# Weight pieces issued from ScalarE, four under way, with five slots in the second layer

## The chip, the cores and the metric

The kernel runs on one core of a Trainium2 chip. The metric is the device time of one execution in microseconds (us); the time before is the median of three runs. The engines of the core are TensorE (PE, with its weight loads as PEld), VectorE (DVE), ScalarE (ACT), GpSimd (POOL) and SyncE (SP). They run side by side, each through its own list of instructions in order, and wait for each other through semaphores. Transfers (DMA) are issued from such a list too, and sixteen DMA engines carry them out.

## The reference

What is computed is a causal attention with a decay, and a two-layer network on its output. Inputs have batch 8, 8 heads, 576 positions and head size 64; the network has model width 512 and inner width 2048, on 8 x 576 = 4608 tokens.

```python
def _attn_ref(q, k, v, f):
    scores = scale * np.matmul(q, k.transpose(0, 1, 3, 2))
    cum = np.cumsum(np.log(np.clip(f, 0.0001, 1.0)), axis=-1)
    decay = cum[:, :, :, None] - cum[:, :, None, :]
    scores = np.where(causal, -1000000000.0, scores + decay)
    attn = np.exp(scores - np.max(scores, axis=-1, keepdims=True))
    attn = attn / (np.sum(attn, axis=-1, keepdims=True) + 1e-09)
    return np.matmul(attn, v)

def _moe_ref(x, w_in, w_out):
    h = x @ w_in
    g = h * np.clip(h + 3.0, 0.0, 6.0) / 6.0
    return g @ w_out
```

`x` is the attention's output with the heads put side by side. The two weights come as 64-bit floats, so each is 8 MB.

## The kernel before

**Attention.** It goes over "virtual heads" (list `VH`): four of kind A, which do the first 256 positions of two heads of batch 0 each; eight of kind B, which do the other positions of one head of batch 0; and 56 of kind F, one head each of batches 1 to 7. For each, q and k come into `ST` (`load_x`, L402), are cut into two parts of fewer bits by GpSimd (`parts`, L441, and `rests`, L451, which also sends T<-TQ and T<-TK through DMAs), and rows of the running sums of the decay come into `TK` (`load_c`). For kinds A and B, `natural` (L474) computes scores for the row maxima, `max_rows` (L495) turns the maxima and sends them as a short row to partition 96 of `TQ` (TQ<-mr, L502), and `scores` (L541) computes transposed scores and exponentials. `av` (L679) multiplies by v. `load_v` (L349) loads v of a batch: batch 0 goes into memory of `v16` and `xT`, the other batches into `vst`. The first load of `vst` stands in the program at the seventh head of kind B.

**The two layers.** Tokens are worked on in nine tiles of 512. `h_unit` (L772) makes 128 of the 2048 inner columns: twelve matmuls (L781 to L783), a Relu on ScalarE (L791), a product on VectorE (L794), and the split of the result into a 16-bit float and a rest (L795, L796). `out_unit` (L799) does the second layer, three matmuls (L803 to L805) for each of 16 chunks. Tile 0 is done in two halves of 256 tokens. These units are woven among the attention's steps by `fill`.

**Weights.** Both weights come in 16 pieces of 512 KB each (128 rows of 512 64-bit numbers). A piece is loaded into a slot (`w_load`, L233). `w_decode` (L241) makes 32-bit floats of it: a pass on ScalarE (L250), two on VectorE (L251, L252), and a Square on ScalarE (L256) that writes over the slot and sums the squares. The Square is the last pass over the slot. When all squares of a group of four pieces (first layer) or of all 16 (second layer) are summed, `pow2_scale` gives a scale, and `w_split` (L281) makes two 16-bit floats of each number: the first on ScalarE (L283), the second through TensorE (L286, L287) and ScalarE (L288) or on VectorE (L294).

The first layer has six slots: the three tiles of `ring`, and three pieces of the memory of `w2`, which is not yet in use. The second layer has three, `ring` alone. Later `ring` serves the heads of kind F.

All loads are issued by SyncE. In the first layer four pieces are loaded ahead, then a fifth, and then piece k + 5 is issued ahead of the decode of piece k; the first eight are pinned behind the last of the short rows issued so far (`pinned`, L206). In the second layer three pieces are loaded ahead, in a step of their own, and then piece k + 3 behind the decode of piece k.

**What sets the order.** The program text gives each instruction a place; the steps of the weights (`w_step`) are put among the attention's, eight to a head of kind A, five for B, four for F (`W_RATE`). A planner then simulates the program and sets each engine's list, by place in the program and by when it takes an instruction to be ready, so that instructions can move against the program text. `tc.issue_after` holds an instruction behind a given one on its engine, and `tc.keep_in_program_order` behind the one traced before it on its engine.

Of the kernel before, what the change touches and what calls it, by code (L numbers as in the profile page):

```python
# [13 lines left out]
I32 = mybir.dt.int32  # L14
# [6 lines left out]
def kernel(  # L21
# [10 lines left out]
    nc = tc.nc  # L32
# [52 lines left out]
    F_RATE = (0.6, 0.45, 1.02)  # L85
    PIN = 0
    PIN0 = 1
# [13 lines left out]
    NSP = 3  # L101
    PL_POOL = ((3, ), ())
    NAT = ((1, 4, 0), (2, 3))
    B0_POOL = ((0, 0), (1, 1))
    W_AHEAD = (4, 5)
    W_ORDER = 0
# [24 lines left out]
    vst = cpool.tile([P, NCH, VR], F32, name="vst")  # L131
# [74 lines left out]
    def pinned():  # L206
        return tc.issue_after(small[-1]) if small else nullcontext()


    wide = w_in.dtype == mybir.dt.int64  # L210
    NW = 16
    CW = NCC * DFF // NW
    wsum = cpool.tile([P, 2 * NW], F32, name="wsum")
    ring = [cpool.tile([P, 2 * CW], I32, name=f"ring{i}") for i in range(NRING)]
    gTf = gT.bitcast(F32).rearrange("p a c t -> p (a c t)")
    w2f = w2.bitcast(F32).rearrange("p k a e -> p (k a e)")
    spare = w2.bitcast(I32).rearrange("p k a e -> p (k a e)")
    slots_out = [t[:, :] for t in ring]
    slots_in = slots_out + [spare[:, (2 * h + 9) * CW:(2 * h + 11) * CW] for h in range(NSP)]

# [11 lines left out]

    def w_load(i, k, slots):  # L233
        src, x, _ = w_chunk(i, k)
        with pinned() if PIN or i == 0 and k < 8 else nullcontext():
            if wide:
                nc.sync.dma_start(slots[k % len(slots)], src.bitcast(I32))
            else:
                nc.sync.dma_start(x, src)

# [55 lines left out]
    def w_in_work():  # L296
        first, ahead = W_AHEAD
        for k in range(first):
            w_load(0, k, slots_in)
        yield  # L300
        for k in range(first, ahead):
            w_load(0, k, slots_in)
        for j in range(NG):
            ks = range(j * NCC, (j + 1) * NCC)
            for k in ks:
                if k + ahead < NW:
                    w_load(0, k + ahead, slots_in)
                w_decode(0, k, slots_in)
                yield
            pm = w_gram(ks) if GRAM[j] else w_sum(ks[0], ks[-1] + 1)  # L310
# [13 lines left out]
    def w_out_work():  # L324
        n = len(slots_out)
        for k in range(n):
            w_load(1, k, slots_out)
        yield

        for k in range(NW):  # L330
            w_decode(1, k, slots_out)
            if k + n < NW:
                w_load(1, k + n, slots_out)
            yield
# [579 lines left out]
    for i, (kind, n) in enumerate(VH):  # L914
        b, h = divmod(n, H)
# [4 lines left out]
        ahead = i + 2 < NV  # L920
# [99 lines left out]
```

## Time and profile before

| what | value |
|---|---|
| median of three runs | 1080.63 us (1080.21 to 1082.72) |
| the profiled execution: time | 1083.28 us |
| the profiled execution: span | 1081.5 us |
| mean granted clock of TensorE | 0.982 |
| PE busy | 1010.1 us (93%) |
| DVE busy | 719.7 us (67%) |
| ACT busy | 610.1 us (56%) |
| POOL busy | 413.1 us (38%) |
| read from HBM | 47.93 MB |

A profile is of one execution. L250 is line 250 of the kernel. The busy time of TensorE includes time in which its pipelined matmuls only overlap. SPq is SyncE's list, where a row is the issuing of a transfer, not its flight. In the chain of waits, a row with DMA is the time from an issue to its landing, as far as it released what follows. A name such as `w` stands for all tiles whose names differ in numbers only: `w1` and `w2` are both `w`. "ring<-in_w_out_dram" is a piece of the second layer's weights on its way into a slot.

### The profile page before, as it was taken

Reading aid. Unit: us, or ns where it says so; the run is one execution under the profiler, and the core shown is the slowest. Engines: PE = TensorE matmul, PEld = TensorE weight load, DVE = VectorE, ACT = ScalarE, POOL = GpSimd, SP = SyncE. Lnnn points to the kernel's source line nnn. Section 1 sums busy time; section 2 is a strip of 40 time slices with the busy share of each in tenths; the row PEclk is TensorE's granted clock in tenths of the full one; section 3 lists DMA queues with packets and bytes.
Section 4 is the critical chain, followed back from the end, with each engine's and each line's share of the span. In section 5 each row is a group of like instructions: output and inputs, shape, how many; then the busy total and the mean of one; then the engine's idle time right before and its main releaser. Section 6 shows DMA issues by size and latency. Waiting matters only on the chain.

```text
span 1081.5 us, 20281 instructions
## 1 busy us (share of the span) xinstructions
PE 1010.1 (93%) x7074; PEld 577.4 (53%) x7074; DVE 719.7 (67%) x1887; ACT 610.1 (56%) x1285; POOL 413.1 (38%) x505
## 2 busy tenths in 40 slices
PE   2799977988999999999999989999999999999998
PEld 2567854755555555555555545555555555444443
DVE  7869899876885688468865795689668841510520
ACT  4778656845764577356754674477447841621520
POOL 7344455335434445444544444454445420000000
PEclk9989989999999999999999999999999999999999
DMA  8866547767756666667576856675666651000001
GB/s 258 277 172 194 150 105 134 179 127 150 156 114 141 140 146 118 137 129 164 108 139 138 164 113 130 146 166 114 128 140 128 106 112 46 1 10 30 1 1 39
DMA packets 261650, 133.74 MB, mean 124 GB/s; under 512 B 229444, under 2 KB 231036, under 8 KB 261548
## 3 DMA queue, kind: packets, MB, share of 16 engines
q1 hardware_dynamic: 261548, 132.45, 54.7%
q8 instruction: 56, 0.92, 0.3%
q14 instruction: 46, 0.38, 0.1%
HBM read 47.93 MB, written 9.73 MB: 53 GB/s over the span
## 4 chain that ended last, share of the span: by engine, by line
PE 64%; DVE 12%; DMA 9%; issue 5%; ACT 5%; SPq 2%; POOL 2%; DVEq 0%; POOLq 0%; ACTq 0%
PE po L803 10%; PE po L804 10%; PE po L805 10%; PE ph L781 7%; PE ph L782 7%; PE ph L783 7%; DMA vst<-in_vS_dram 3%; PE pn L611 3%; PE pn L608 2%; DVE pp L619 2%; DVE ring L648 2%; DMA T<-TK 1%; DVE gT L796 1%; DMA w<-in_w_in_dram 1%; DVE r L794 1%
## 5 line engine op out<-in xcount | busy, mean ns | idle before, releaser
L781 PE MATMUL ph<-xT,w 128*128 128x512 f16 (+1 forms) x640 | 231.2, 363 | 14.5 <-DVE r L794 9.1
L782 PE MATMUL ph<-xT,w 128*128 128x512 f16 (+1 forms) x640 | 230.2, 363 | 0.0
L783 PE MATMUL ph<-xT,w 128*128 128x512 f16 (+1 forms) x640 | 230.0, 363 | 0.0
L631 ACT ACTIVATE pp<-pp,nb 128x192 f32<-128x192 f32 x280 | 138.5, 552 | 148.8 <-DVE nb L625 145.8
L804 PE MATMUL po<-w,gT 128*128 128x512 f16 x576 | 216.3, 381 | 6.1 <-DVE w L294 6.1
L805 PE MATMUL po<-w,gT 128*128 128x512 f16 x576 | 215.9, 381 | 0.0
L803 PE MATMUL po<-w,gT 128*128 128x512 f16 x576 | 213.6, 381 | 1.1 <-ACT o L814 0.8
L648 DVE TENSOR_TENSOR ring<-pp,ring 128x128 f16<-128x128 f32 (+2 forms) x216 | 131.5, 622 | 84.1 <-ACT ring L645 83.2
L791 ACT ACTIVATE r<-ph,bias_r,SC 128x256 f32<-128x256 f32 (+7 forms) x272 | 144.4, 570 | 28.6 <-PE ph L783 27.9
L794 DVE SCALAR_TENSOR_TENSOR r<-r,ph 128x512 f32<-128x512 f32 (+1 forms) x160 | 100.1, 627 | 88.9 <-ACT r L791 88.6
L458 POOL TENSOR_TENSOR T<-ST,T 64x576 fp32r<-64x576 f32 (+1 forms) x68 | 101.2, 1488 | 143.2 <-DMA T<-TK 133.4
L619 DVE CUSTOM_DVE_ANT_0 pp<-pn,W 128x192 f32<-128x192 f32 x280 | 122.9, 482 | 20.6 <-PE pn L611 16.6
L796 DVE TENSOR_TENSOR gT<-r,gT 128x512 f16<-128x512 f32 (+1 forms) x160 | 118.3, 743 | 27.4 <-ACT gT L795 26.6
L795 ACT CAST gT<-r 128x512 f16<-128x512 f32 (+1 forms) x160 | 91.8, 575 | 75.9 <-DVE r L794 75.8
L608 PE MATMUL pn<-TK,TQ 68*128 68x192 f32 x336 | 124.1, 383 | 5.8 <-issue 5.0
L611 PE MATMUL pn<-T,T 128*128 128x192 f32 x336 | 113.5, 368 | 4.3 <-POOL T L458 4.3
L645 ACT CAST ring<-pp 128x192 f16<-128x192 f32 x280 | 112.9, 452 | 0.0
L455 POOL TENSOR_TENSOR T<-ST,TQ 64x576 fp32r<-64x576 f32 (+2 forms) x68 | 97.6, 1435 | 24.8 <-PE pn L611 18.2
L654 POOL TENSOR_TENSOR ring<-pp,ring 128x128 f16<-128x128 f32 x96 | 61.5, 641 | 105.5 <-ACT ring L645 83.7
L782 PEld LDWEIGHTS <-w 128*128 128x128 f16 x640 | 62.7, 99 | 65.8 <-issue 20.9
L805 PEld LDWEIGHTS <-gT 128*128 128x128 f16 x576 | 56.8, 99 | 74.9 <-issue 13.7
L781 PEld LDWEIGHTS <-w 128*128 128x128 f16 x640 | 63.1, 99 | 62.2 <-issue 14.3
(136 smaller groups left out, 1703.4 us busy)
## 6 DMA issues: line engine op xcount, KB each, us to landing
ST<-in_qk_dram SPq DMA_DIRECT2D x64, 288.0 KB
T<-TK SPq DMA_DIRECT2D x64, 144.0 KB
out_dram<-o SPq DMA_DIRECT2D x36, 256.0 KB
ring<-in_w_out_dram SPq DMA_DIRECT2D x16, 512.0 KB
T<-TQ SPq DMA_DIRECT2D x56, 144.0 KB
vst<-in_vS_dram SPq DMA_DIRECT2D x7, 1040.0 KB
ring<-in_w_in_dram SPq DMA_DIRECT2D x9, 512.0 KB
w<-in_w_in_dram SPq DMA_DIRECT2D x7, 512.0 KB
```

What stands on the lines that cost most here:

```text
L608: nc.tensor.matmul(dst, TQ[i][0:D + 4, qs], TK[i][0:D + 4, a:e], start=True, stop=False)
L611: nc.tensor.matmul(dst, T7[j][:, qs], T1[j][:, a:e], start=False, stop=True)
L619: nc.vector.tensor_tensor_reduce(pp[:r, w:w + kw], pn[:r, o:o + kw], W[:r, 4 * P + r - kw:4 * P + r], 1.0, -3.0e38, ALU.add, ALU.max, accu ...
L631: nc.scalar.activation(x_, x_, AF.Exp, bias=nb[:r, e0 + x:e0 + x + 1], scale=0.125)
L648: eng.tensor_tensor(hl[:r, a:a + c * P], pp[:r, at[c] + 64:at[c] + kw], hl[:r, h0[c] + 64:h0[c] + kw], op=ALU.subtract,)
L781: nc.tensor.matmul(ph, w1[0][:, cc, fs_], xh, start=(cc == 0), stop=False)
L782: nc.tensor.matmul(ph, w1[0][:, cc, fs_], xl, start=False, stop=False)
L783: nc.tensor.matmul(ph, w1[1][:, cc, fs_], xh, start=False, stop=(cc == NCC - 1))
L791: nc.scalar.activation(r[:, a:e], ph[:, a:e], AF.Relu, bias=bias_r, scale=scol(A1 + NG * b + fc * NG // NFC))
L803: nc.tensor.matmul(po, gT[:, 0, fc, ts_], w2[:, fc, 0, :], start=(fc == 0), stop=False)
L804: nc.tensor.matmul(po, gT[:, 0, fc, ts_], w2[:, fc, 1, :], start=False, stop=False)
L805: nc.tensor.matmul(po, gT[:, 1, fc, ts_], w2[:, fc, 0, :], start=False, stop=(fc == NFC - 1))
```

## The change

- Only the first four loads are issued by SyncE. Each later one is issued by ScalarE, traced behind the decode of a piece: all 32 pieces of both layers form one list, and each decode takes the next from it. So the load of piece k + 4 stands behind the Square of piece k, and the first four pieces of the second layer stand behind the decodes of the last four of the first.
- `tc.keep_in_program_order` holds each of ScalarE's loads behind the instruction traced ahead of it on ScalarE, which is the Square.
- The pinning of the first eight loads behind the short rows, the fifth load ahead, and the step in which the second layer's first three loads were issued are taken out.
- The second layer has five slots: `ring`, and two in the memory of `vst`. The first load of `vst` therefore has to wait for the last use of these two.

```diff
-    W_AHEAD = (4, 5)
+    W_AHEAD = 4
...
-    slots_out = [t[:, :] for t in ring]
-    slots_in = slots_out + [spare[:, (2 * h + 9) * CW:(2 * h + 11) * CW] for h in range(NSP)]
+    vsp = vst.bitcast(I32).rearrange("p c e -> p (c e)")
+    slots_out = [t[:, :] for t in ring] + [vsp[:, 2 * h * CW:2 * (h + 1) * CW] for h in range(2)]
+    slots_in = [t[:, :] for t in ring] + [spare[:, (2 * h + 9) * CW:(2 * h + 11) * CW] for h in range(NSP)]
...
-    def w_load(i, k, slots):
+    loads = [(i, k) for i in range(2) for k in range(NW)]
+
+    def w_load(eng):
+        if not loads:
+            return
+        i, k = loads.pop(0)
         src, x, _ = w_chunk(i, k)
-        with pinned() if PIN or i == 0 and k < 8 else nullcontext():
-            if wide:
-                nc.sync.dma_start(slots[k % len(slots)], src.bitcast(I32))
-            else:
-                nc.sync.dma_start(x, src)
+        slots = (slots_in, slots_out)[i]
+        dst, src = (slots[k % len(slots)], src.bitcast(I32)) if wide else (x, src)
+        d = eng.dma_start(dst, src)
+        if eng is nc.scalar:
+            tc.keep_in_program_order(d)
...
     def w_in_work():
-        first, ahead = W_AHEAD
-        for k in range(first):
-            w_load(0, k, slots_in)
+        for k in range(W_AHEAD):
+            w_load(nc.sync)
         yield
-        for k in range(first, ahead):
-            w_load(0, k, slots_in)
         for j in range(NG):
             ks = range(j * NCC, (j + 1) * NCC)
             for k in ks:
-                if k + ahead < NW:
-                    w_load(0, k + ahead, slots_in)
                 w_decode(0, k, slots_in)
+                w_load(nc.scalar)
                 yield
...
     def w_out_work():
-        n = len(slots_out)
-        for k in range(n):
-            w_load(1, k, slots_out)
-        yield
-
         for k in range(NW):
             w_decode(1, k, slots_out)
-            if k + n < NW:
-                w_load(1, k + n, slots_out)
+            w_load(nc.scalar)
             yield
```

More of the change, by code (lines that the diff above doesn't have):

```diff
@@ L85 @@
     F_RATE = (0.6, 0.45, 1.02)
-    PIN = 0
     PIN0 = 1
```

## The prediction

> **What bounds the kernel now.** I first read the busy times in five stretches of the span, then who TensorE waits for up to 135 us, then the timelines around its longest holes, and last the chain of work that ended last.
>
> A row of the windows gives the stretch, its length, busy time (and instructions) of PE, PEld, DVE, ACT, POOL, then the granted clock, the DMA share and GB/s.
> ```profile
> span 1081.5 us, 20281 instructions
> ...
> 10.00:54.00 44.00, 26.69 (x115) 20.32 (x115) 34.30 (x106) 26.08 (x58) 21.22 (x27) 0.95 0.88 270
> 54.00:136.00 82.00, 77.97 (x556) 62.55 (x557) 65.83 (x183) 59.14 (x125) 36.73 (x39) 0.94 0.58 170
> 136.00:200.00 64.00, 49.86 (x443) 33.23 (x444) 62.52 (x173) 44.34 (x95) 33.95 (x35) 0.95 0.66 138
> ...
> 300.00:1081.00 781.00, 764.18 (x5257) 403.86 (x5255) 473.10 (x1205) 413.67 (x865) 269.50 (x335) 1.00 0.50 105
> ```
> From 300 us on TensorE is busy 764 of 781 us and no weight piece is under way, so the change can't act there except by an order of work that starts earlier or later. From 54 to 136 us it is busy 78.0 of 82. From 136 to 200 VectorE is busy 62.5 of 64 us, and TensorE idles 14.1. The room that touches weight loading is the stretch from 10 to 54 us: 17.3 us idle on TensorE, and its longest two waits up to 135 us are these (total, times, longest):
> ```profile
> PE pn L484 <- DMA TK<-cs: 12.8, 1, 12.8
> PE ps L548 <- DMA TQ<-mr: 7.4, 2, 4.3
> ```
> The 12.8 are the start of the attention and no weight's business. The 7.4 are two waits for a 2 KB row of maxima. The later one is the last row of TensorE's timeline here, and then come issues on SyncE's queue:
> ```profile
> 47.94 0.38 PE L183 MATMUL pt_w<-wm,ones 128*128 128x1 f32 x2 [2.50 <-ACT w L288]
> ...
> 53.04 0.27 PE L499 MATMUL ptm<-identr,MC 128*3 128x128 f32 x1 [1.77 <-DVE MC L490]
> 56.38 0.58 PE L548 MATMUL ps<-TQ,TK 97*128 97x256 f32 x1 [3.07 <-DMA TQ<-mr]
> ```
> ```profile
> 42.39 0.52 SPq L237 DMA_DIRECT2D ring<-in_w_in_dram  x1
> ...
> 46.01 0.33 SPq L237 DMA_DIRECT2D ring<-in_w_out_dram  x1
> ...
> 48.07 0.67 SPq L502 DMA_DIRECT2D TQ<-mr  x1
> ```
> From the first to the second of these rows SyncE issues four weight pieces of 512 KB (the page's list of issues has the size), all in one queue ahead of that small row. The chain says what it costs (start, length, what):
> ```profile
> 14.40 7.06 DMA w<-in_w_in_dram
> 24.99 6.42 DMA w<-in_w_in_dram
> 42.39 4.33 DMA ring<-in_w_in_dram
> 48.07 8.26 DMA TQ<-mr
> 77.89 5.30 DMA ring<-in_w_out_dram
> 90.48 3.96 DMA ring<-in_w_out_dram
> ```
> Up to 95 us the chain runs five times through the flight of a weight piece, 27.1 us in all, and once through 8.26 us for the small row. So early on the kernel is paced by when weight pieces and the small transfers queued among them land.
>
> **The change, part by part.** *SyncE loses 28 of its 32 weight issues, and ScalarE gains them* (four remain on SyncE at the start). Their issues now, by the view of each weight's tile (duration in ns min/median/max):
> ```profile
> L237 SPq DMA_DIRECT2D ring<-in_w_in_dram x9: 327/432/534, 2.0 to 44.8; - x9
> ...
> L237 SPq DMA_DIRECT2D ring<-in_w_out_dram x16: 323/420/1287, 32.8 to 110.7; - x16
> ```
> 28 x 0.42 = 11.8 us leave SyncE, and with them the time in which SyncE stood before a piece whose slot wasn't free, while the attention's transfers queued behind it (from 0 to 200 us):
> ```profile
> SPq L237 <- ACT ring L256: 5.9, 6, 2.0
> SPq L237 <- ACT w L256: 3.3, 2, 2.0
> ```
> The small row of 48.07 us is then in a queue that holds no weights ahead of it. Weight pieces now fly 3.96 us where the queue is shortest (the chain's 90.48), so I expect no more than that of a row of 2 KB: 8.26 - 3.96 = 4.3 us sooner, more than the 3.07. The 1.77 just ahead are a wait for the maxima of the next head, on a VectorE that stands behind the same stall's decodes. I take both, **-4.8 us**. Bounds: -4.84, and 0 if the row is as late as now.
> The Trainium skill ("DMA: Bandwidth & Descriptors", "Queues, rings and completion order") says that each DMA engine takes turns between the queues of SyncE and ScalarE, a packet at a time. By that, the row passes the weights and the term stands; the trace of before has one data queue and cannot show it.
>
> *The clock.* Behind that stall TensorE runs slowly:
> ```profile
> 50.00:60.00 10.00, 5.17 (x22) 4.45 (x22) 4.52 (x20) 6.92 (x14) 3.03 (x3) 0.50 0.68 175
> 60.00:70.00 10.00, 10.00 (x46) 6.11 (x45) 6.80 (x24) 7.09 (x16) 4.11 (x6) 0.84 0.41 119
> ...
> 40.62 0.36 PE L548 MATMUL ps<-TQ,TK 97*128 97x256 f32 x1
> ```
> The matmul of 56.38 us takes 0.58 where the same took 0.36 at 40.62. From 56.4 to 60 us that is 3.6 x 0.38 = 1.4, and 10 x 0.16 = 1.6 in the next ten: 3.0 us if the clock never fell, 0 if it falls all the same. Some idle time will stay there, so half: **-1.5 us**.
>
> *Pieces start earlier.* The fifth to eighth piece are no longer held behind the attention's small transfers: each goes out behind the Square of one of the first four, where now the sixth issue is at 14.40 and the eighth at 24.99 (the chain's first two rows). ScalarE now idles for landings:
> ```profile
> ACT gT L250 <- DMA ring<-in_w_in_dram: 10.2, 6, 5.3
> ACT gT L250 <- DMA w<-in_w_in_dram: 5.3, 3, 2.4
> ACT w L250 <- DMA ring<-in_w_out_dram: 3.9, 5, 1.5
> ...
> 46.74 0.66 ACT L250 ACTIVATE gT<-ring 128x512 f32<-128x512 f32 x1 [0.76 <-DMA ring<-in_w_in_dram]
> ```
> Little of these 19.4 us is on TensorE's path. The one place I can point to is TensorE's 2.50 at 47.94, which waited for an eviction (L288) that stands right behind this decode of 46.74 on ScalarE, and so behind its 0.76. **-0.8 us**; bounds 0 and -2.5. That more pieces are under way doesn't raise the rate where the DMA share is full already:
> ```profile
> 20.00:30.00 10.00, 6.92 (x32) 6.42 (x32) 8.64 (x25) 3.82 (x8) 4.32 (x5) 1.00 1.03 320
> ...
> 19.09 0.43 SPq L354 DMA_DIRECT2D v<-in_vS_dram  x1
> ...
> 24.35 1.75 DVE L365 TENSOR_REDUCE vm<-v 128x1 f32<-128x1536 f32 x1 [0.20 <-DMA v<-in_vS_dram]
> 25.91 2.88 PE L702 MATMUL pav<-v,pf 128*128 128x96 f32 x12
> ```
> There the weights take it from v and the heads. The load of v, issued at 19.09 and landed by 24.35, could at half the rate need 5.3 us more and hold the matmuls of L702, at 25.91 now, by 24.35 + 5.26 - 25.91 = 3.7. Against that, the first small row (the 4.3 of the 7.4) may come sooner by up to half, 2. I take 0, bounds -2 and +3.7.
>
> *ScalarE pays the issues.* 28 x 0.42 = 11.8 us. From 10 to 136 us ScalarE is idle 17.9 + 22.9 = 40.8, which covers them. Behind an issue on ScalarE stand the exponentials (L567), the evictions (L288, L791) and the next decode, and TensorE and VectorE wait for these. Only three issues add a wait: output pieces 0 to 2 go into the slot that the Square just ahead of them has written. Later ones use a slot whose readers were done one piece before. On the path I count those of the stretch from 44 to 56 us, where TensorE is not covered: three, **+1.3 us**. Bounds 0 and 11.8 (if none were covered).
>
> *Five slots in the second layer.* Two lie in vst, so the load of batch 1's v must now wait for the Square of output piece 14 of 0 to 15. At present the last Square but one runs at 113.65 and the load is issued behind a small row of 115.33:
> ```profile
> 113.65 0.63 ACT L256 ACTIVATE ring<-w 128x512 f32<-128x512 f32 x1 [0.26 <-DVE w L252]
> ...
> 115.33 0.75 SPq L502 DMA_DIRECT2D TQ<-mr  x1
> ```
> 1 us of slack as it is, more if the pieces come sooner: 0. If they come later by x, VectorE (which reduces that v) loses x - 1. Decoding earlier gains nothing by itself from 54 to 136 us, where TensorE has 4.0 us of idle left, 3.07 of them already counted; nor from 136 on, where VectorE has the same passes to do: 0.
>
> Sum: -4.8 - 1.5 - 0.8 + 1.3 = **-5.8 us**. The profiled execution took 1083.28 us (span 1081.5), 2.65 above the median of 1080.63; it becomes 1077.5, and the median **1074.8**.
>
> **The rivals.** *A, more:* the second layer's pieces are decoded early enough that VectorE's splits of them also move ahead. TensorE waits for the splits in 136 to 200 us:
> ```profile
> PE po L804 <- DVE w L294: 6.1, 5, 1.8
> ```
> All of it: -5.8 - 6.1 = -11.9, 1068.7. For it: VectorE idles 16.2 us from 54 to 136, room for earlier passes. Against: the splits stand in the program behind steps of the attention.
> *B, nothing:* sharing 16 engines, the small row is as late as now, and the stall with its slow clock stays; -0.8 + 1.3 = +0.5, 1081.1. For it: the share of 1.03 in 20 to 30 us; four weight pieces are always under way, in rows of 512 KB / 128 = 4 KB. Against: in 54 to 136 us the share is 0.58.
> The skill's same page ("Issuing engines are not separate DMA queues") says that issuing from several engines only saves sequencer time, which is B's outcome.
> *C, slower:* ScalarE's issues land on the path. An issue takes up to 1.287 us on SyncE, and ScalarE's stream is in order, so exponentials and evictions come late by the issue and the wait before it. If all 28 count at 0.42: +11.8 - 7.1 = +4.7, 1085.3. It decides from 10.3 us on the path (7.1 gained, 3.2 lost): 25 issues at 0.42, or 8 at 1.287. For it: ScalarE is busy 59.1 of 82 us, in series with VectorE at 65.8. Against: the idle time above. That the whole order is planned anew, and may fall worse, is in the range.
>
> **Chances.** Forecast 0.37, A 0.18, B 0.20, C 0.25. No change is within 0.3% (3.2 us), about what a measurement of this kernel can tell. Forecast and A are faster: 0.55; B the same: 0.20; C slower: 0.25. The likeliest's own range is 1071 to 1078; for 8 in 10 it goes from 1066 (A, with the earlier v and eviction bounds) to 1086 (C).
>
> **What would show it.** A second data queue with some 28 x 512 KB in the page's third section. TensorE's wait for TQ<-mr near 50 us gone and that row landing within 4 us of its issue; the clock in 50 to 70 us above 0.8. ScalarE's waits for weight landings well under 19.4 us, and the last Square of the second layer before 118 us. A is right if L804 no longer waits for L294. C is right if TensorE shows new waits for L567, L288 or L791 that add up to more than 7 us. The prediction is wrong if v lands after 28 us and L702 waits for it, or if the span changes behind 300 us, where I count nothing.

## The result and the profile after

The changed kernel takes 1095.9 us (median; 1093.49 to 1100.15), the kernel before beside it 1081.68 us. The ratio is **1.0129**, 95% interval 1.0085 to 1.0173: the change makes the kernel 1.3% slower. A second measurement of the same change, with more runs, gave 1.0125 (1.0087 to 1.0163). The prediction was 1074.8 us, with a range up to 1086.

In the changed kernel every line behind L400 or so has a number lower by 3 than before: L564 is the exponential (before L567), L699 the product with v (L702), L481 the scores for the maxima (L484), L545 the transposed scores (L548). The weights' loads are at L244, the passes of a decode at L257 to L259 and its Square at L263.

The page of the changed kernel, its span and its queues:

```profile
span 1091.7 us, 20269 instructions
...
q1 hardware_dynamic: 257516, 117.77, 49.2%
q10 hardware_dynamic: 4032, 14.68, 4.6%
```

The second data queue is there: 14.68 MB are 28 pieces of 512 KB. The profiled execution took 1093.49 us, and its span is 10.2 us longer than that of before.

Where the 10.2 us are: the windows view, first of the kernel before and then of the changed one. A row gives the stretch, its length, the busy times (and instructions) of PE, PEld, DVE, ACT and POOL, TensorE's granted clock, the DMA share and GB/s.

```profile
0.00:60.00 60.00, 30.32 (x130) 23.66 (x131) 44.22 (x135) 36.12 (x74) 33.16 (x49) 0.91 0.83 253
60.00:136.00 76.00, 74.35 (x542) 59.21 (x542) 63.83 (x175) 54.47 (x117) 33.70 (x37) 0.98 0.58 174
```

```profile
0.00:60.00 60.00, 24.45 (x100) 17.82 (x100) 42.14 (x122) 32.95 (x68) 31.70 (x46) 0.97 0.84 255
60.00:136.00 76.00, 74.15 (x487) 59.56 (x488) 57.38 (x164) 52.28 (x109) 29.27 (x33) 0.87 0.59 164
...
300.00:1091.00 791.00, 773.48 (x5313) 409.14 (x5311) 477.05 (x1215) 419.78 (x879) 272.62 (x341) 0.99 0.50 106
```

Busy time times clock is the work that TensorE did, in us at full clock. Up to 60 us it was 30.32 x 0.91 = 27.6 before. In the changed kernel the slow clock falls into 56 to 60 us, when TensorE does nothing (a row further below), so its work is all of the 24.45: 3.1 behind. From 60 to 136 us it was 72.9 before and 64.5 after: 8.4 more, although TensorE is busy as long as before (74.15 of 76 us). That part is clock alone. At 136 us the changed kernel is some 11 us behind. Behind 300 us TensorE idles 791 - 773.5 = 17.5 us, against 16.8 before, at a granted clock of 0.99 against 1.00: little happened there.

Over the whole span TensorE's idle time (span less busy time) grew from 71.4 to 76.2 us, and the work that the slow clock took, added up from windows of 2 us, from 14.2 to 20.1. These 4.8 and 5.9 us make up the 10.2 within half a us: idle time and slow clock have like parts in the loss.

TensorE's waits up to 136 us in the changed kernel (total, times, longest):

```profile
PE pn L481 <- DMA TK<-cs: 12.9, 2, 12.4
PE pav L699 <- ACT pf L564: 6.9, 1, 6.9
PE pn L481 <- ACT pf L564: 6.4, 2, 5.9
PE ptm L496 <- DVE MC L487: 5.4, 1, 5.4
...
PE ps L545 <- DMA TQ<-mr: 1.1, 1, 1.1
```

The waits put down to the small row of maxima fell from 7.4 to 1.1 us. Two waits are new, both for an exponential on ScalarE (L564), together 13.3 us. A third grew: that for maxima from VectorE (L487), which was 3.1 us in three waits before.

The fall from 7.4 to 1.1 is only in part what the change was predicted to bring. The first product with the first small row, before and then after:

```profile
22.20 0.58 PE L548 MATMUL ps<-TQ,TK 97*128 97x256 f32 x1 [4.30 <-DMA TQ<-mr]
```

```profile
23.44 0.27 PE L496 MATMUL ptm<-identr,MC 128*4 128x128 f32 x1 [5.45 <-DVE MC L487]
24.78 0.58 PE L545 MATMUL ps<-TQ,TK 97*128 97x256 f32 x1 [1.08 <-DMA TQ<-mr]
```

It starts 2.6 us later, and the idle time ahead of it has another name: VectorE decodes pieces between the maxima that TensorE waits for. From issue to landing, the rows of the four heads of kind A took 3.8, 5.3, 5.9 and 8.3 us before, and 5.4, 3.2, 3.8 and 3.3 us after. So the first row got slower and the other three faster. The wait of 3.07 us at 56.38 is gone.

The chain of waits of the changed kernel leads through both waits for an exponential (start, length, what):

```profile
13.78 8.34 DMA ring<-in_w_in_dram
...
22.14 10.95 DMA xT<-in_vS_dram
...
33.11 0.33 ACTq L244
...
33.49 0.91 ACT pf L564
...
34.44 2.88 PE pav L699 x12
...
50.18 6.81 DMA ring<-in_w_out_dram
```

And ScalarE's own timeline, where the number in brackets is its idle time ahead and what ended it:

```profile
33.11 0.33 ACTq L244 DMA_DIRECT2D ring<-in_w_in_dram  x1
33.49 0.90 ACT L564 ACTIVATE pf<-ps,bias_p 128x768 f32<-128x768 f32 x1 [5.67 <-DMA xT<-in_vS_dram]
...
57.01 0.66 ACT L257 ACTIVATE w<-ring 128x512 f32<-128x512 f32 x1 [2.54 <-DMA ring<-in_w_out_dram]
57.57 0.58 ACT L295 ACTIVATE w<-low 128x512 f16<-128x512 f32 x1
59.02 0.67 ACT L257 ACTIVATE w<-ring 128x512 f32<-128x512 f32 x1 [0.86 <-DMA ring<-in_w_out_dram]
59.25 0.34 ACTq L244 DMA_DIRECT2D vst<-in_w_out_dram  x1
59.58 0.89 ACT L564 ACTIVATE pf<-ps,bias_p 128x768 f32<-128x768 f32 x1
```

**The first stall, S.** One part of v (xT<-in_vS) is issued at 22.14 and flies 10.95 us. An exponential doesn't need v at all, yet it starts only behind that landing. What stands ahead of it is ScalarE's issue of a weight piece at 33.11. In the trace that issue waits for one semaphore only, the one that this transfer of v counts up when it lands. The two queues' transfers use eight such semaphores in turn, so an issue can't go out before the eighth transfer ahead of it, counted over both engines, has landed; seven others are issued between 22.14 and 33.11. It holds the other way round, too. One of the waits of SyncE's list up to 60 us:

```profile
SPq L352 <- DMA ring<-in_w_in_dram: 1.1, 1, 1.1
```

L352 is the issue of this part of v. It stood 1.1 us for a piece that ScalarE had issued at 13.78, the first row of the chain above.

The decodes and Squares ahead of ScalarE's issue were done at 27.8 us. TensorE got the exponential at 34.44, after 6.95 us without work. The part of v that its matmuls read landed at 31.1 us, so 3.6 of the 6.95 were due to v itself. The other 3.3 came by way of ScalarE's issue.

**The second stall, D.** From 54 to 59 us ScalarE decodes the first pieces of the *second* layer, which at this rate of loading come under way at 48 us. It waits 2.54 and 0.86 us for their landings, with an exponential behind them that is on TensorE's path. TensorE waits 5.92 us for it.

**The clock behind D.** Windows of the changed kernel, then one of before:

```profile
56.00:60.00 4.00, 0.00 (x0) 0.00 (x0) 2.23 (x7) 2.13 (x4) 0.00 (x0) 0.51 0.88 303
60.00:70.00 10.00, 9.47 (x33) 7.24 (x34) 8.08 (x31) 9.55 (x21) 3.90 (x4) 0.51 0.94 285
84.00:92.00 8.00, 8.00 (x29) 5.96 (x30) 6.35 (x17) 5.86 (x13) 3.22 (x6) 0.50 0.89 204
```

```profile
84.00:92.00 8.00, 7.94 (x65) 6.74 (x63) 7.93 (x21) 7.27 (x16) 3.80 (x4) 1.00 0.54 153
```

TensorE idles all of 56 to 60 us and then works at half clock up to 70 us. A second stretch at half clock, from 84 to 92 us, has no counterpart before. 9.47 x 0.49 + 8.00 x 0.50 = 8.6 us of work are lost in the last two rows; before lost 10 x 0.16 = 1.6 in the same places. But before had its slow clock earlier, and lost 30.32 x 0.09 = 2.7 us by it up to 60 us, where the changed kernel lost next to nothing.

### The profile page after: what moved, and what is told of

Read it like the earlier page. It is cut to its first block, busy times and chain, and to the rows that moved or that the text cites. A ratio compares the mean times of both kernels' runs of the same rounds, so it can differ in the third digit from the quotient of the medians.

```text
span 1091.7 us, 20269 instructions
## 1 busy us (share of the span) xinstructions
PE 1015.5 (93%) x7074; PEld 580.9 (53%) x7074; DVE 713.0 (65%) x1887; ACT 610.3 (56%) x1285; POOL 415.1 (38%) x505
## 3 DMA queue, kind: packets, MB, share of 16 engines
q10 hardware_dynamic: 4032, 14.68, 4.6%
## 4 chain that ended last, share of the span: by engine, by line
PE 72%; DMA 9%; DVE 8%; ACT 5%; issue 3%; SPq 2%; POOL 1%; ACTq 0%; DVEq 0%; POOLq 0%
PE po L800 10%; PE po L801 10%; PE po L802 10%; PE ph L778 9%; PE ph L779 9%; PE ph L780 9%; PE pn L608 3%; PE pn L605 3%; PE pav L699 2%; DVE pp L616 2%; DMA vst<-in_vS_dram 2%; DMA ring<-in_w_out_dram 2%; PE pav L692 1%; ACT pp L628 1%; PE pav L693 1%
## 5 line engine op out<-in xcount | busy, mean ns | idle before, releaser
L645 DVE TENSOR_TENSOR ring<-pp,ring 128x128 f16<-128x128 f32 (+2 forms) x216 | 129.3, 613 | 85.0 <-ACT ring L642 82.4
L793 DVE TENSOR_TENSOR gT<-r,gT 128x512 f16<-128x512 f32 (+1 forms) x160 | 114.2, 718 | 29.6 <-ACT gT L792 29.0
L642 ACT CAST ring<-pp 128x192 f16<-128x192 f32 (+1 forms) x280 | 113.2, 452 | 0.4 <-DMA pT<-ring 0.4
```

Source lines behind the costliest of these rows:

```text
L645: eng.tensor_tensor(hl[:r, a:a + c * P], pp[:r, at[c] + 64:at[c] + kw], hl[:r, h0[c] + 64:h0[c] + kw], op=ALU.subtract,)
```

## The experiments

Three theories stood at the start. **S**: at the start the pieces take the transfers from v, and the exponentials and the products with v come late. **D**: the second layer's pieces are decoded too early, ahead of exponentials that TensorE needs. **L**: issues on ScalarE are the trouble, since each waits for the eighth transfer ahead and holds what stands behind it.

### The first layer's part alone

```diff
-    slots_out = [t[:, :] for t in ring] + [vsp[:, 2 * h * CW:2 * (h + 1) * CW] for h in range(2)]
+    slots_out = [t[:, :] for t in ring]
...
-    loads = [(i, k) for i in range(2) for k in range(NW)]
+    loads = [(0, k) for k in range(NW)]
...
     def w_out_work():
+        n = len(slots_out)
+        for k in range(n):
+            w_issue(nc.sync, 1, k)
+        yield
+
         for k in range(NW):
             w_decode(1, k, slots_out)
-            w_load(nc.scalar)
+            if k + n < NW:
+                w_issue(nc.sync, 1, k + n)
```

`w_issue` loads a given piece. The second layer is loaded as before, by SyncE into three slots.

> Only the first layer's loads are moved to ScalarE; the second layer's stay on SyncE with three slots. Measured so far: 1081.7 before, 1095.9 changed, 14 us apart. Theory S (the loss is made at the start: the weights' own queue takes the DMA engines from the load of v, VectorE and ScalarE stand behind v, and TensorE waits some 7 us for the exponential at 34 us): the loss is nearly all here, 1088 to 1096. Theory D (the loss is made in the second layer: pieces are decoded ahead of the exponentials and ScalarE waits in order for their landings, some 6 us at 60 us): little of the loss is here, 1081 to 1085.

Measured: 1.0041 (1.0023 to 1.0060), a median of 1086.5 us, between the two ranges. S's wait is there nearly in full, 5.5 us for the same exponential. From 60 to 136 us, 9.8 us are lost to idle time and slow clock (before 3.1), 6.5 of them clock. Yet the span of the profiled execution is only 1.1 us longer than that of before: the rest is made up elsewhere.

### The second layer's part alone

```diff
-    loads = [(i, k) for i in range(2) for k in range(NW)]
+    loads = [(1, k) for k in range(NW)]
...
-        for k in range(W_AHEAD):
-            w_load(nc.sync)
+        def first(k):
+            if k < NW:
+                with pinned() if k < 8 else nullcontext():
+                    w_issue(nc.sync, 0, k)
+
+        for k in range(4):
+            first(k)
         yield
+        first(4)
...
+                first(k + 5)
                 w_decode(0, k, slots_in)
-                w_load(nc.scalar)
+                if k >= 12:
+                    w_load(nc.scalar)
```

`first` issues a first-layer piece on SyncE, pinned as before.

> Only the second layer's loads are moved to ScalarE, with the five slots; the first layer's are as in the kernel before. Theory S: no v load is harmed, 1078 to 1083. Theory D: 1086 to 1094. If the two losses add, this and the first-layer run together come to some 14 us.

Measured: 1.0020 (1.0000 to 1.0039), which can hardly be told from no change; the 1083.7 us are just above S's range and below D's. Five slots, and sixteen issues on ScalarE, don't cost the 1.3% by themselves. The two parts alone add up to 0.6%, not 1.3%: together they cost more than apart. How the one adds to the other's loss is not shown. With the first layer's pieces at their old times, TensorE's longest wait for an exponential is 1.2 us.

### The same places, all issued by SyncE

```diff
-                w_load(nc.scalar)
+                w_load(nc.sync)
```

(in both layers)

> All loads stand in the program where the change has them, with its five slots, but SyncE issues them all, so they share a queue with the attention's transfers and are not held behind the Square on ScalarE. Theory L (an issue waits until the eighth transfer ahead of it has landed, since eight completion semaphores are used in turn, and on ScalarE this wait stops the computing): most of the loss goes, 1079 to 1085. Theory S in its plain form (four pieces under way early are too much for the DMA engines, whoever issues them): the loss stays, 1090 to 1098.

Measured: 1.0159 (1.0128 to 1.0191). The expectation of theory L fell: without a single issue on ScalarE the loss is as large. SyncE's queue shows why this is no better. The planner sets SyncE's list, and a load whose slot has no earlier user can go first of all:

```profile
7.00 1.67 SPq L244 DMA_DIRECT2D vst<-in_w_out_dram  x2
...
28.83 0.38 SPq L351 DMA_DIRECT2D v<-in_vS_dram  x1
```

Two pieces of the second layer, which nothing needs for 50 us, go out at 7 us, and v at 28.83 instead of 19.09. TensorE's first wait grows from 12.8 to 17.6 us. Whoever issues, pieces too early take the transfers from what is needed first. But since this kernel has a fault of its own, it doesn't show that ScalarE's issues cost nothing in the change.

### The first eight pieces held as before

```diff
         for k in range(W_AHEAD):
             w_load(nc.sync)
         yield
+        with pinned():
+            w_load(nc.sync)
...
+                if k < 3 and j == 0:
+                    with pinned():
+                        w_load(nc.sync)
                 w_decode(0, k, slots_in)
-                w_load(nc.scalar)
+                if j:
+                    w_load(nc.scalar)
```

> As the change, but the first eight pieces are loaded as before: by SyncE, behind the short rows of the attention; ScalarE issues from the ninth piece on. Theory S: v lands by 25 us again, the 7 us wait at 34 us goes, 1083 to 1089. Theory L: ScalarE still stands at other issues; half or more of the loss stays, 1089 to 1096.

Measured: 1.0027 (1.0008 to 1.0047), 1085.4 us, as S has it. The windows of 20 to 40 us, of this kernel and of the changed one:

```profile
20.00:40.00 20.00, 16.34 (x62) 12.70 (x62) 13.48 (x45) 11.15 (x22) 9.12 (x10) 1.00 0.91 294
```

```profile
20.00:40.00 20.00, 7.19 (x31) 6.34 (x31) 12.01 (x31) 8.33 (x19) 6.34 (x6) 1.00 0.84 279
```

TensorE is busy 16.34 us in place of 7.19 (before: 15.94). The first product with the small row starts at 20.07 us (before 22.20). So the stall of the first 60 us comes from the fifth to eighth piece at their early places. The edit takes more away than S, though. Up to 136 us TensorE waits for no exponential at all, so D's wait is gone with it. And ScalarE no longer issues these four pieces, so the late v and the issue that waits for it aren't told apart.

### Issues on ScalarE alone

```diff
+    mark = cpool.tile([P, 4 * NW], I32, name="mark")
...
+        if NW * i + k < 2 * NW - 4:
+            c = 2 * (NW * i + k)
+            d = nc.scalar.dma_start(mark[:, c:c + 2], w_out[0:P, 0:1].bitcast(I32))
+            tc.keep_in_program_order(d)
```

The kernel before, with a transfer of 1 KB that nothing uses behind the Squares of 28 pieces.

> The kernel before, with 28 transfers of 1 KB each added, issued by ScalarE behind the Squares of the first 28 pieces, where the change issues its loads; the weights stay on SyncE. It carries the cost of the issues on ScalarE alone (28 x 0.34 us, and the wait of each for the eighth transfer ahead of it), without any weight moved. Theory L (issuing on ScalarE is what costs): 1086 to 1092. Theories S and D (what costs is which pieces are under way when): 1079 to 1085.

Measured: 1.0035 (1.0009 to 1.0061), 3.8 us for 28 issues of 0.335 us (the median on ScalarE). The 1086.5 us are at the lower end of L's range. Two kernels below, with no added instruction at all, show 1.0022 and 1.0032, so little of the 3.8 need be the issues' own. How long an issue stands depends on the transfers around it, and these transfers of 1 KB leave the pieces where they were.

### v ahead of the fifth piece

```diff
     load_x(1)
+    load_v(0)
...
     load_x(2)
-    load_v(0)
```

The changed kernel, with the load of v right behind the first four pieces.

> The change, with the load of the first v issued by SyncE right behind the first four pieces, and not behind the first short row at 19 us. Theory S with v as the victim: VectorE no longer waits 4.1 us for v, TensorE's 6.95 us at 34 us go, and the time falls by 5 to 9 us against the change, to 1087 to 1091. If v is only one of several transfers that suffer, the next one takes its place: 1092 to 1098.

Measured: 1.0063 (1.0034 to 1.0092), 1091.9 us, about 1 above the range for v as the victim. S's wait of 6.95 us is gone, D's too, and 20 to 40 us look as in the run with the eight pieces held:

```profile
20.00:40.00 20.00, 16.45 (x72) 10.32 (x73) 18.14 (x62) 14.98 (x31) 8.43 (x9) 1.00 0.93 266
```

The start is now ahead of the kernel before (32.24 x 0.93 = 30.0 us of work by 60 us, against 27.6), although TensorE's first wait grew from 12.8 to 16.2 us. But from 200 to 300 us 22.7 us are lost to idle time and clock, against 13.2 before. The gain is given back later.

### The second layer's loads behind the first layer's work

```diff
-    loads = [(i, k) for i in range(2) for k in range(NW)]
+    loads = [(0, k) for k in range(NW)]
...
     def w_out_work():
+        loads.extend((1, k) for k in range(NW))
+        for k in range(W_AHEAD):
+            w_load(nc.sync)
+        yield
```

> The change, with the second layer's first four pieces issued only behind the whole first layer (by SyncE, in a step of their own as in the kernel before), the rest by ScalarE, five slots. The first layer is as changed. Theory D (the loss beyond that of the first layer comes from second-layer pieces that are issued and decoded ahead of the exponentials at 50 to 60 us): as the run with the first layer alone, 1084 to 1089. If the five slots or ScalarE's later issues are what adds the loss: 1091 to 1097.

Measured: 1.0049 (1.0021 to 1.0078), 1088.6 us, as D has it. Besides S's wait, which is still 6.9 us, the longest for an exponential is 3.4. So taking D's cause away helps, without S being touched.

### The kernel before with v ahead

The edit of v, made to the kernel before.

> The kernel before with the load of v in the same early place. It shows what that move does by itself. In the kernel before VectorE waits 0.2 us for v, so theory S expects 1080 to 1084, no change; a gain or loss of 4 us and more would say that the place of v matters by way of the order of work and not of its landing.

Measured: 1.0018 (0.9994 to 1.0042): no gain. In the kernel before v was not late.

### Both suspects out

The edits of "the first eight pieces held" and "the second layer's loads behind the first layer's work" together, in the changed kernel.

> The change with both suspects taken out: the first eight pieces loaded as before by SyncE behind the short rows, and the second layer's first four pieces issued only behind the whole first layer. ScalarE issues the other 20, and the second layer has its five slots. Each alone brought the change from a ratio of 1.013 to 1.003 (held) and 1.005 (later). If S and D are the whole loss: 0.997 to 1.003 of the kernel before. If issuing on ScalarE costs by itself, as the added small issues did (ratio 1.0035): 1.003 to 1.006.

Measured: 1.0115 (1.0086 to 1.0145). This contradicts a plain sum of S and D, by which it should have been near 1. The two waits are gone and the first 60 us are 6.9 us better than before (35.55 x 0.97 = 34.5 us of work). Then 15.7 us are lost from 60 to 136 us, where before lost 3.1. Over the whole span TensorE idles no longer than before (71.1 us against 71.4); the slow clock took 23.0 us of work, against 14.2. So 8.8 of the 11.7 us that this span is longer are clock. SyncE's list shows a second-layer piece in vst issued at 6.14 us here, and one at 5.71 us in the run with the second layer's loads later, which lost only 0.5%.

### Five slots alone

```diff
-    slots_out = [t[:, :] for t in ring]
-    slots_in = slots_out + [spare[:, (2 * h + 9) * CW:(2 * h + 11) * CW] for h in range(NSP)]
+    vsp = vst.bitcast(I32).rearrange("p c e -> p (c e)")
+    slots_out = [t[:, :] for t in ring] + [vsp[:, 2 * h * CW:2 * (h + 1) * CW] for h in range(2)]
+    slots_in = [t[:, :] for t in ring] + [spare[:, (2 * h + 9) * CW:(2 * h + 11) * CW] for h in range(NSP)]
```

The kernel before: all loads at their old places on SyncE, and the second layer with two more slots.

> The kernel before with nothing but the second layer's five slots; SyncE issues all loads at their old places, five pieces ahead in the second layer. ScalarE waits 3.9 us for second-layer landings in the kernel before. If more slots help by themselves: 0.995 to 0.998. Theory D (pieces that come earlier are decoded ahead of what TensorE needs): 1.001 to 1.006.

Measured: 1.0133 (1.0094 to 1.0171), outside both ranges. As much as the whole change, from a part that I had priced at nothing. SyncE's timeline of this kernel:

```profile
5.94 1.11 SPq L238 DMA_DIRECT2D vst<-in_w_out_dram  x2
9.02 2.86 SPq L428 DMA_DIRECT2D TK<-cs  x4
...
18.05 0.74 SPq L238 DMA_DIRECT2D vst<-in_w_out_dram  x1
...
19.26 0.36 SPq L238 DMA_DIRECT2D vst<-in_w_out_dram  x1
...
23.05 0.38 SPq L355 DMA_DIRECT2D v<-in_vS_dram  x1
```

vst has no user until batch 1's v, so the planner takes these loads as ready at once and sends them before the rows that start the attention, and before v. TensorE's first wait is 16.2 us in place of 12.8. In the changed kernel the same loads are held in ScalarE's list (the first vst load goes out at 52.98 us), so this mechanism is not the change's own. With the same five slots and ScalarE's issues, in the second layer's part alone, the ratio was 1.0020. What this kernel shares with S is that weight pieces are in flight while the first transfers are wanted.

### Two pieces under way

```diff
-    W_AHEAD = 4
+    W_AHEAD = 2
```

> The change with two pieces under way in place of four. Theories S and D: half the pieces compete with v and the heads, and the second layer's pieces come later; ratio 1.000 to 1.006. Theory L (ScalarE's issues and their waits are the cost): the issues are two more, and the ratio stays at 1.009 and more.

Measured: 1.0157 (1.0125 to 1.0189). Here S and D missed, and L's number held, though not by L's way. Fewer in flight is no cure. The waits for exponentials are gone (0.5 us is left up to 136 us), and 21.6 us are lost from 136 to 200 us, where before lost 16.6. Over the whole span TensorE idles 8.9 us more than before and loses 2.0 less to the slow clock, which is 6.9 of the 11.7 us; where the rest is, these traces don't show.

### The change again

> The change itself once more, beside these runs on the same chip, since its ratio of 1.0129 rests on four runs: 1.009 to 1.015. If it comes out at 1.007 or less, the differences to the single-cause runs are within their intervals, and S and D can't be told apart by times.

Measured: 1.0125 (1.0087 to 1.0163). Both waits are there, 4.87 us at 33.62 and 5.71 us at 58.38.

### The loading or the written order?

With both suspects out and the loss still there, another reading had to be excluded: that any small edit makes the planner write another order of the work, and that the change merely drew a bad one (theory **P**), against the loading as the cause (**W**). These four kernels move one number of the planner's estimate by 5%, in the kernel before and in the changed one. No instruction is added or taken away.

```diff
-    H_COST = 1.05
+    H_COST = 1.1
```

(and 1.0 in the "low" ones)

> The kernel before with one number of the planner's estimate moved by 5% (H_COST 1.05 to 1.10): no instruction is added or removed, only the written order of the engines' work changes. Theory P (any small edit makes the planner write another order, and another order alone costs as much as the change): ratio to before 1.004 to 1.013, with slow clock in 60 to 136 us of over 5 us, as in all the experiments so far (before 1.5). Theory W (the way the weights are loaded costs it): ratio within 0.3% of 1.

> The same with the estimate moved the other way (H_COST 1.05 to 1.00). Theory P: ratio 1.004 to 1.013, and differing from e14 by 0.3% or more, since the order is a draw. Theory W: within 0.3% of 1, like e14.

> The changed kernel with H_COST 1.10. Theory P: the changed kernel's 1.0129 is one draw of an order among those that the experiments gave, so this one falls to 1.002 to 1.008, or at least moves by 0.4% or more. Theory W: 1.010 to 1.016, with the two waits of TensorE (6.95 us at 34 us behind the late exponential, 5.9 us at 60 us) still there.

> The changed kernel with H_COST 1.00. Theory P: between 1.002 and 1.012, differing from e16 by 0.3% or more. Theory W: 1.010 to 1.016, as e16. If e14 and e15 are near 1 and e16 and e17 near 1.013, the loading is the cause whatever the order; if the four lie between 1.002 and 1.013 without regard to which kernel they come from, the order is.

Measured: before with other orders 1.0022 (0.9994 to 1.0050) and 1.0032 (1.0003 to 1.0061); the change with other orders 1.0124 (1.0089 to 1.0159) and 1.0146 (1.0108 to 1.0185). Theory P fell, in the form in which these four kernels try it. Such an order costs 0.2 to 0.3%, and the change costs 1.2 to 1.5% in each of three orders. It also follows that a ratio of 1.002 to 1.003 in the runs above can be the order alone. The waits go the same way. TensorE's, of the change with the higher estimate:

```profile
PE pn L481 <- ACT pf L564: 5.3, 2, 4.8
PE pav L699 <- ACT pf L564: 5.0, 1, 5.0
```

and of the kernel before with the higher estimate, where the largest wait for an exponential is

```profile
PE pn L484 <- ACT pf L567: 0.2, 1, 0.2
```

The windows, of the kernel before with the higher estimate and then of the change with it:

```profile
0.00:60.00 60.00, 31.84 (x130) 25.36 (x131) 44.34 (x134) 35.62 (x73) 32.91 (x49) 0.90 0.84 253
60.00:136.00 76.00, 74.31 (x544) 59.64 (x544) 64.39 (x175) 54.42 (x117) 33.51 (x37) 0.99 0.58 174
```

```profile
0.00:60.00 60.00, 27.02 (x109) 19.88 (x109) 45.96 (x127) 34.74 (x72) 31.73 (x46) 0.96 0.86 259
60.00:136.00 76.00, 74.36 (x485) 58.60 (x484) 57.51 (x162) 51.38 (x107) 29.45 (x33) 0.87 0.59 164
```

Work done by 136 us, added up from windows of 2 us: 100.3, 101.5 and 99.4 us in the three orders of the kernel before; 89.0, 89.5, 90.8 and 90.8 in the four traces of the change (its second trace among them). The means are 10.4 us apart, and those of the seven spans 8.9. Such a lag isn't a loss by itself: the kernel before with v ahead has done 92.6 us by then, and the one with the first layer's part alone 92.4, and their spans are only 1.0 and 1.1 us longer than that of before.

### Five slots, and both suspects out, in another order

`H_COST = 1.0` in the kernels of "five slots alone" and "both suspects out".

> The kernel before with the second layer's five slots alone (as e11, loads at their old places on SyncE) and H_COST 1.00 in place of 1.05, so that only the written order differs from e11. e14 and e15 moved before by 0.2 to 0.3% this way, e16 and e17 moved the change by less than 0.2%. If the slots' edit costs by what it loads when, the ratio stays at 1.0133, within 0.4%. If e11 drew a bad order, it falls to 1.002 to 1.008.

> e10 (v ahead of the fifth piece and ScalarE's start free of issues, the second layer's loads behind the first layer's work) with H_COST 1.00 in place of 1.05. If undoing both suspects leaves a cost that belongs to the loading, the ratio stays at 1.0115, within 0.4%. If e10 drew a bad order, it falls to 1.002 to 1.008, near e4 and e7, which undid one suspect each.

Measured: 1.0143 (1.0107 to 1.0178) and 1.0094 (1.0059 to 1.0128). Neither was a bad draw. Five slots on SyncE cost 1.3 to 1.4% by what they load when. And undoing both stalls by these edits leaves about 1%. Why isn't settled: a piece goes into vst at 6 us here too, but the first 60 us are the best of all in one of these orders. So each of the two edits alone brought a gain, and both together hardly any; a kernel free of both that keeps the change's gain was not found, and none of the kernels here beats the one before.

## Why the prediction was wrong

**"SyncE loses 28 of its 32 weight issues", -4.8 us.** Right in its place: the row there flew 8.26 us and now flies 3.3, and the 3.07 at 56.38 is gone. For the first row, which was to come sooner by up to 2, it was wrong: the product with it starts 2.6 us later. The Trainium skill ("DMA: Bandwidth & Descriptors", "Queues, rings and completion order") says that a DMA engine takes turns between the queues. The trace agrees in this case: the row issued at 59.55 landed at 62.8, ahead of the piece that ScalarE had issued at 59.25, which landed at 63.7.

**"Pieces start earlier", -0.8, and "I take 0, bounds -2 and +3.7".** This is the first of the steps that failed; "Five slots" and "The clock" below are the others. I named the load of v, worked out what half the rate would do to it, and chose 0 because the first small row might gain as much. The product with it came 2.6 later instead. And v did get half the rate: the part issued at 20.59 let VectorE start at 31.13, 10.5 us later, where before it took 5.26. ScalarE issues weight pieces at 18.26, 20.71, 23.36 and 24.76, around v's issues from 20.59 to 22.73. The issue of this part, and VectorE's reduction of it, where before it waited 0.20:

```profile
20.59 0.39 SPq L351 DMA_DIRECT2D v<-in_vS_dram  x1
```

```profile
31.13 1.75 DVE L362 TENSOR_REDUCE vm<-v 128x1 f32<-128x1536 f32 x1 [4.12 <-DMA v<-in_vS_dram]
```

The wait was 6.95 us, more than the 3.7, because v held more than the matmuls that read it. Those account for 3.6, the bound that I had worked out. The other 3.3 came through ScalarE: its issue had to wait for the landing of another part of v, and an exponential stood behind it. The pinning that the change takes out is what had kept these pieces behind the short rows. With v ahead, or with the eight pieces held, the first 60 us were better than before. With the pieces held the first row gained the 2 that I had hoped for (20.07 against 22.20).

**"ScalarE pays the issues", +1.3, bounds 0 to 11.8.** The price of an issue was about right: 0.33 us each, and at most 3.8 us for 28 in the run that adds small ones. What I left out is what an issue *waits* for. I counted only waits for a slot ("only three issues add a wait"), and the wait that cost most was for an unrelated transfer. I named the exponentials as the ones that stand behind, and didn't ask what else could hold the issue.

**"Five slots", 0.** "Decoding earlier gains nothing by itself" held, but it was the wrong question: it *costs*. The last second-layer decode came at 94 us instead of 116, and the first ones, at 54 to 59 us, stand ahead of an exponential for which TensorE waits 5.92 us. The early second-layer pieces are part of the loss: with them issued later the ratio falls to 1.0049. That run keeps the five slots, so what it saves is the price of issuing and decoding the first of these pieces early. The load of batch 1's v, which I took for the risk here, paid nothing: vst was free at 98 us, the load goes out at 124.69, and VectorE waits 1.78 us for it where it waited 1.45.

**"The clock", -1.5.** Wrong in sign. Over the whole span the slow clock took 5.9 us more than before. I expected the stall at 50 to 56 us to go and the clock to hold. The stall moved to 54 to 60 us, with another cause, the clock fell all the same, and it fell a second time. From 60 to 136 us that is 9.6 us of lost work against 1.5 before, of which the 2.7 that before lost up to 60 us must be taken off. That the first slow stretch follows on D's idle time is in the rows above. What brings on the second one at 84 us is not settled: TensorE idled only 1.1 us in 82 to 84.

**The rivals.** C was the right one in sign, and passed the mark that I gave it: new waits for L564 add up to 13.3 us, over 7. Its mechanism was half right. "Exponentials come late by the issue and the wait before it" is what the trace shows at 33 us; that all 28 issues count at their own length is not, and 1085.3 is 10.6 us short of the result. A fell: TensorE's wait for the splits from VectorE is 7.2 us over the whole span, against 6.1. B fell as a time (1081.1), but sharing told in part as it says: the first small row was no sooner, and a stall with slow clock behind it was there again.

**The marks.** The second data queue carried the 28 pieces, the row behind the old stall landed 3.3 us after its issue, and the last Square of the second layer ran at 98 us. The clock of 50 to 70 us was not above 0.8: it was 0.80 up to 60 us and 0.51 behind it. ScalarE's waits for weight landings fell from 19.4 to 12.2 us, in three rows:

```profile
ACT w L257 <- DMA ring<-in_w_out_dram: 5.4, 4, 2.5
ACT gT L257 <- DMA w<-in_w_in_dram: 3.5, 3, 1.5
ACT gT L257 <- DMA ring<-in_w_in_dram: 3.3, 4, 1.7
```

So even the aim, more pieces under way, was reached, and TensorE gained nothing by it that shows. I wrote that the prediction is wrong "if v lands after 28 us and L702 waits for it": v landed at 31 us.

**What is shown and what isn't.** Idle time of TensorE over the whole span, and the work that the slow clock took (from windows of 2 us), in one profiled execution of each kernel:

| kernel | span, us | idle | slow clock |
|---|---|---|---|
| before | 1081.5 | 71.4 | 14.2 |
| the change | 1091.7 | 76.2 | 20.1 |
| the first layer's part alone | 1082.6 | 71.8 | 14.4 |
| the first eight pieces held | 1085.6 | 71.8 | 17.9 |
| v ahead | 1090.3 | 71.7 | 27.5 |
| the second layer's loads later | 1087.7 | 72.4 | 19.3 |
| both suspects out | 1093.2 | 71.1 | 23.0 |

Shown: the loss stays with the change in three written orders (seven traces, three of them of the kernel before). The fifth to eighth piece at their early places make the stall of the first 60 us, and without them there the ratio falls from 1.0129 to 1.0027. Neither layer's part costs much alone; the loss takes both. Each cure of one stall brings TensorE's idle time back to about that of before, and what it leaves is slow clock. Issues on ScalarE are not needed for a loss of this size. Argued from the trace only: that D's wait starts the first stretch of slow clock, and that in S the late v and ScalarE's issue share the wait as 3.6 and 3.3. Open: what brings on the second stretch, why the two parts together cost more than apart, and why the kernel with both suspects out loses so much to the clock.

## What to carry to other kernels

Before prefetching more, list what else is in flight in the same stretch, and who reads it first: a transfer that gets half the rate is late by its own length, and pays on every engine that waits behind it. An issue on a compute engine is a wait of that engine for everything the issue depends on, the completion semaphores of unrelated transfers among them, so put it only where nothing urgent stands behind. Two parts that cost 0.4% and 0.2% alone cost 1.3% together, so try them together before you add them up. And a new, empty slot is an invitation: a planner may fill it at the very start, when the transfers are wanted elsewhere.

## What was not expected of the hardware

**Transfers of two engines hold each other through shared semaphores.** With eight in turn for both queues, ScalarE's issue at 33.11 us waited for SyncE's transfer of 22.14, and that one had waited for ScalarE's piece of 13.78, which landed at 22.12. This is the program's doing, not the queues'. The queues can pass each other, as the row of 59.55 did, but they share the rate: v took 10.5 us between pieces, and 5.26 before.

**Half clock while fully busy.** From 84 to 92 us TensorE is busy 8.00 of 8 us at a granted clock of 0.50, behind 1.1 us of idle time in two. The Trainium skill ("TensorE: Matmul & The Clock Gate", "Part 1: The HAM clock gate (the "warmup" mystery)") has the full clock back after about 3.4 us of work, and lost after an idle window of that length. Here it took some 10 us to come back (from 92 to 94 us the clock is 0.59, with TensorE busy all of it), and the gap ahead of it was shorter. The same part of the page also tells of a kernel whose clock swings with many short gaps, which is nearer. The measurement decides for this kernel. Not each such gap brings it on: from 72 to 74 us the second trace of the change shows 0.72 us of idle time and keeps the full clock.
